# Result stored feature-major, range checks without clips, an inverse root on GpSimd, token-major inputs and a plan driven by need

## The chip, the cores and the metric

The kernel runs on one core of one Trainium2 chip. The metric is the device time of one execution in microseconds (us), the median of several runs. A core has a matrix engine (TensorE, PE in the profile, with its weight loads as PEld), a vector engine (VectorE, DVE), an engine for functions (ScalarE, ACT), a fourth compute engine (GpSimd, POOL) and the engine that issues the DMAs of this kernel (SyncE, SP).

## The reference, cut to what matters

Two blocks in a row. The first is a linear attention whose state decays by a complex factor; the second is a gated block with a product over time.

```python
# attention: q, k, v, a_re, a_im are [batch 4, heads 8, seq 768, dim 48]
mag = sqrt(a_re**2 + a_im**2);  scale = minimum(mag, 0.999) / (mag + 1e-6)
a = (a_re + i*a_im) * scale
S = 0                                    # [batch, head, 48, 48], complex
for t in range(768):
    S = a[t][:, None] * S + outer(k[t], v[t])
    y[t] = q[t] @ real(S)
x = y laid out as [4, 768, 384]          # heads side by side
# gated block: w_in [384, 1024], w_sg [768, 768], w_out [512, 384]
u, v = split(gelu(x @ w_in), 2)          # 512 each
v_n = (v - mean(v)) / sqrt(var(v) + 1e-6) * g_ln
v_s = w_sg @ v_n + b_sg                  # over time, for each batch
result = x + (u * v_s) @ w_out           # [4, 768, 384]
```

## The kernel before, in words

**Tiling.** Time is cut in 24 chunks of 128 tokens (6 for each batch), and chunks are taken in 13 *units* of one or two. For each unit a row of steps runs, each a Python function or generator: `load` (re, im, q, k; L227), `square` (re² + im², L255), `logs` (L273), `scale` (the cumulative decay as a product with a triangular matrix, then exponentials on q and k, L298), `arctan` and `turns` (the cumulative phase, L331 and L342), `sincos` (L374), `rotate` (q and k times cosine and sine, on DVE, L383), and for each chunk `attend` (L392).

**attend.** It transposes Q and K on PE (`pq`, `pk`, L407), evacuates them on ACT (`qt`, `kt`), multiplies them (`pa`, L415), masks the result on DVE (`am`, L417: one for each four heads, so two a chunk, which makes `am` a good counter of chunks), updates the state (`ps`, L424), forms the output (`py`), evacuates it on ACT (`yp`) and stores it feature-major in a scratch array `xd`.

**The gated block.** It runs for each batch in three halves of 256 tokens (the code calls them hf). `normal` (L489) loads x from `xd`, splits it in two parts for the three-product matmul `mm3` (L155; a float32 product as high·high + high·low + low·high in fp32r: `xh`, `xl`), forms the v half (`pv`), gelu, mean and variance (L504, L505), the inverse root `rsqrt` (L457, twelve operations on 128x2 elements on DVE), scales and splits (`vh`, `vl`). `expand` (L519) loads x again and forms u (`pu`). `spatial` (L535) needs all three `normal`s of the batch: for each of four f it forms `pvs` (18 matmuls, L158), then on DVE `tg` = pvs·g + b (L546) and `tg`·u, splits it (`gh` on ACT, `gl` on DVE), and then for each of two chunks forms the output product `po` token-major (12 matmuls of 384 columns), transposes x back with three PE transposes (`px`, L565), copies that to `ob` on ACT, adds `po` on DVE (L569) and stores 128 tokens (L570).

**Clips.** `square` begins with two DVE passes: L260 limits re from below and keeps the smallest value (for the range check at the end, `in_range`), and L262 limits im to ±1. If a value lies outside the range in which the fast form holds, a slow general path (`general`) is taken; it isn't in the runs shown.

**Weights.** They arrive as float64 and are turned to two fp32r parts by integer operations on DVE (`fetch`, L167, tiles `raw` and `bits`). w_sg is float32; `prep_sg` (L200) transposes its 36 blocks on PE (`pt_sg`, L210), casts the high part on ACT (L212) and subtracts on DVE (L213).

**What sets the order.** Every step of every unit and half gets a position from a table of numbers W; all steps are sorted by it and called in that order. Each engine works in order through what was written for it, so this sort is the kernel's schedule, and an instruction that is not ready holds everything behind it on its engine. The same holds for SP, which issues all DMAs. Functions on ACT come in three sets, and each change of set is an ACT_TABLE_LOAD (L116).

Where `EN` maps a name to (early, late), the two numbers choose between two engines for units ahead of and from the seventh on. In before all but `rn` are 0.

Of the kernel before, what the change touches and what calls it, by code (L numbers as in the profile page):

```python
# [29 lines left out]
def tile_kernel(ctx: ExitStack, tc: tile.TileContext, q, k, v, a_re, a_im,  # L30
                w_in, g_ln, w_sg, b_sg, w_out, out):
    nc = tc.nc
    B, H, S, D = q.shape
# [41 lines left out]
    mask = u_phi.bitcast(F32)  # L75
    b_eps = cst([P, 1], F32, "b_eps")
    nc.gpsimd.memset(b_eps, LN_2EPS)
# [4 lines left out]
    vbuf = []
    for i in range(2):
        t = cst([P, H, 64], F32, f"vbuf{i}")
        nc.gpsimd.memset(t, 0.0)
# [22 lines left out]
    def act(out, in_, func, bias=None, scale=1.0):  # L108
        kw = {}
# [90 lines left out]
    def prep_sg(tt):  # L200
# [5 lines left out]
        for g in range(2):  # L206
            pt = psm.tile([P, 3, P], F32, tag="m", name="pt_sg")
            for i in range(3):
                s_ = 3 * g + i
                nc.tensor.transpose(pt[:, i, :], st[:, s_ * P:(s_ + 1) * P], ident)  # L210
# [1 line left out]
            nc.scalar.copy(wh, pt)  # L212
            nc.vector.tensor_tensor(out=wl, in0=pt, in1=wh.bitcast(F32), op=ALU.subtract)  # L213
# [568 lines left out]
```

## Time and profile before

| what | number |
|---|---|
| median of 3 runs | 545.34 us (544.06 to 546.47) |
| the profiled execution | 544.33 us |
| its span, first to last instruction | 542.6 us |
| mean granted TensorE clock | 0.967 |
| DMA moved, mean rate | 50.80 MB, 94 GB/s |
| DMA packets, of those under 512 B | 169747, 145997 |

How to read it: the times of instructions are of the one profiled execution, whose own time, 544.33 us, is 1.7 above the span and 1.0 under the median. A group's row gives line, engine, operation, output and inputs with their shapes, the count after x, then the busy time in us and the mean in ns; behind the second bar stands the idle time of that engine just before these instructions, and what ended most of it. "128x512 f32" is 128 partitions by 512 elements.

### The profile page before, as it was taken

How to read it: one execution, taken by the hardware profiler on the slowest of the kernel's cores; microseconds unless marked ns; L12 is line 12 of the kernel's file. 1: busy time of each engine (PE TensorE's matmuls, PEld its weight loads, DVE VectorE, ACT ScalarE, POOL GpSimd, SP SyncE). 2: the span in 40 equal slices, each digit the busy share in tenths (PEclk: the TensorE clock that was granted, in tenths of full speed). 3: DMA queues.
4: the chain of work that ended last, by engine and by line, in shares of the span. 5: the costliest groups of instructions: out<-in, count | busy, mean ns of one | idle time of the engine just before them, and what ended most of it. 6: DMA issues, size and time to landing. Idle time of an engine off the chain costs nothing.

```text
span 542.6 us, 10051 instructions
## 1 busy us (share of the span) xinstructions
PE 488.5 (90%) x3838; PEld 440.0 (81%) x3838; DVE 403.8 (74%) x939; ACT 340.5 (63%) x573; POOL 2.2 (0%) x14
## 2 busy tenths in 40 slices
PE   1759787959899999999998999999999999999994
PEld 0448474747689999998798999998899999889994
DVE  5898889899888869499888587688874433884432
ACT  5879875777859687593599594874682332442221
POOL 1000000000000000000000000000000000000000
PEclk9989798798899999999999999999999999999998
DMA  8687767455552454454322544134221103120101
GB/s 160 177 192 185 181 150 178 85 123 118 117 117 35 103 100 85 121 118 102 103 39 51 124 83 104 45 88 104 72 32 30 59 16 103 31 87 1 59 31 36
DMA packets 169747, 50.80 MB, mean 94 GB/s; under 512 B 145997, under 2 KB 167503, under 8 KB 169690
## 3 DMA queue, kind: packets, MB, share of 16 engines
q1 hardware_dynamic: 169690, 50.07, 40.1%
q8 instruction: 32, 0.52, 0.4%
q14 instruction: 25, 0.20, 0.1%
HBM read 40.58 MB, written 9.47 MB: 92 GB/s over the span
## 4 chain that ended last, share of the span: by engine, by line
PE 68%; DVE 15%; ACT 12%; issue 3%; DMA 1%; SPq 1%; ACTq 0%; DVEq 0%
PE pvs L158 17%; PE pu L158 9%; PE po L158 8%; PE pa L415 7%; PE pv L158 6%; PE py L441 3%; PE ps L424 3%; PE pq L407 3%; PE pk L407 3%; PE py L446 2%; ACT L116 2%; PE px L565 1%; PE phi L357 1%; ACT vh L120 1%; DVE bst L504 1%
## 5 line engine op out<-in xcount | busy, mean ns | idle before, releaser
L158 PE MATMUL pvs<-wsgh,vh 128*128 128x256 f32 x288 | 83.8, 291 | 0.8 <-ACT vh L120 0.8
L158 PE MATMUL pvs<-wsgh,vl 128*128 128x256 f32 x288 | 81.2, 282 | 0.2 <-DVE vl L153 0.2
L158 PE MATMUL pvs<-wsgl,vh 128*128 128x256 f32 x288 | 81.0, 281 | 0.0
L415 PE MATMUL pa<-qt,kt 96*128 96x128 f32 x384 | 56.7, 289 | 9.8 <-ACT kt L143 9.5
L415 PEld LDWEIGHTS pa<-qt,kt 96*128 96x128 f32 x384 | 51.1, 200 | 17.0 <-ACT kt L143 15.2
L116 ACT ACT_TABLE_LOAD x43 | 55.2, 1283 | 1.6 <-PEq L767 0.8
L158 PEld LDWEIGHTS pvs<-wsgh,vh 128*128 128x128 f32 x288 | 54.3, 189 | 1.8 <-ACT vh L120 1.3
L158 PEld LDWEIGHTS pvs<-wsgh,vl 128*128 128x128 f32 x288 | 54.4, 189 | 0.6 <-DVE vl L153 0.5
L158 PEld LDWEIGHTS pvs<-wsgl,vh 128*128 128x128 f32 x288 | 54.4, 189 | 0.0
L120 ACT ACTIVATE gh<-tg 128x256 fp32r<-128x256 f32 x48 | 20.0, 417 | 40.3 <-DVE tg L548 36.6
L569 DVE TENSOR_TENSOR ob<-po,ob 128x384 f32<-128x384 f32 x24 | 13.3, 555 | 41.5 <-ACT ob L143 38.9
L158 PE MATMUL pu<-xh,winh 128*128 128x256 f32 x144 | 43.0, 300 | 0.0
L158 PE MATMUL pu<-xl,winh 128*128 128x256 f32 x144 | 40.8, 284 | 1.3 <-DVE xl L153 1.3
L407 PE MATMUL pq<-ident,Q 128*96 128x128 f32 x192 | 32.7, 295 | 9.7 <-DVE Q L389 9.7
L158 PE MATMUL pu<-xh,winl 128*128 128x256 f32 x144 | 40.4, 282 | 0.0
L441 PE MATMUL py<-am,vbuf 128*64 128x128 f32 x384 | 39.0, 280 | 1.3 <-DVE am L417 0.9
L546 DVE SCALAR_TENSOR_TENSOR tg<-pvs,gcol,bsg 128x256 f32<-128x256 f32 x48 | 23.2, 482 | 20.9 <-PE pvs L158 20.0
L143 ACT COPY qt<-pq 96x512 f32<-96x512 f32 x48 | 27.7, 577 | 17.0 <-PE pq L407 16.7
L417 DVE TENSOR_TENSOR am<-pa,u_phi 128x512 f32<-128x512 f32 x48 | 32.9, 685 | 5.7 <-PE pa L415 5.7
L407 PEld LDWEIGHTS pq<-ident,Q 128*96 128x96 f32 x192 | 22.7, 134 | 15.6 <-DVE Q L389 11.8
L407 PE MATMUL pk<-ident,K 128*96 128x128 f32 x192 | 32.1, 291 | 1.8 <-DVE K L389 0.9
L158 PE MATMUL pv<-winh,xh 128*128 128x512 f32 x72 | 30.8, 428 | 2.8 <-ACT ob L143 1.9
(228 smaller groups left out, 1264.4 us busy)
## 6 DMA issues: line engine op xcount, KB each, us to landing
x<-xd SPq DMA_DIRECT2D x24, 384.0 KB, 3.4
re<-in_a_re_dram SPq DMA_DIRECT2D x24, 192.0 KB, 3.4
im<-in_a_im_dram SPq DMA_DIRECT2D x24, 192.0 KB, 2.6
q<-in_q_dram SPq DMA_DIRECT2D x24, 192.0 KB, 3.2
k<-in_k_dram SPq DMA_DIRECT2D x24, 192.0 KB, 3.7
vbuf<-in_v_dram SPq DMA_DIRECT2D x24, 192.0 KB, 3.1
xd<-yp SPq DMA_DIRECT2D x48, 96.0 KB, 2.2
out_dram<-ob SPq DMA_DIRECT2D x24, 192.0 KB, 2.0
```

What stands on the lines that cost most here:

```text
L116: p = nc.scalar.preload_act_table_set(SETS[t])
L120: i = nc.scalar.activation(out, in_, func, scale=scale, **kw)
L143: nc.scalar.copy(out, in_)
L158: nc.tensor.matmul(o, w(i), x(i), start=(i == 0 and j == 0), stop=(i == n - 1 and j == 2))
L407: nc.tensor.transpose(pp[:, hh, :], x[:, 4 * g2 + hh, :, :].rearrange("p a d -> p (a d)"), ident)
L415: nc.tensor.matmul(pa[:, hh, :], kt[:, hh, :], qt[:, hh, :], start=True, stop=True)
L417: nc.vector.tensor_tensor(out=am, in0=pa, in1=mask.unsqueeze(1).broadcast_to([P, 4, P]), op=ALU.mult)
L424: nc.tensor.matmul(ps[:, h, :], K[:, h, :, :].rearrange("p a d -> p (a d)"), V[:, h, 0:D], start=True, stop=True)
L441: nc.tensor.matmul(py[64 * e:64 * e + 64, p_, :], V[:, h, :], am[:, h % 4, :], start=True, stop=c == 0)
L446: nc.tensor.matmul(py[64 * e:64 * e + D, p_, :], Sb[:, h, :], qt[:, h % 4, :], start=False, stop=True)
L546: nc.vector.scalar_tensor_tensor(out=tg, in0=pv, scalar=gcol[:, f:f + 1], in1=bsg[:, tsl], op0=ALU.mult, op1=ALU.add)
L569: nc.vector.tensor_tensor(out=ob, in0=po, in1=ob, op=ALU.add)
```

## The change

The host now hands in q, k, re, im as [batch, seq, 384] (token-major, as the kernel's tiles are), v padded to 64 a head and w_sg transposed, and transposes the result, which the kernel now stores feature-major as [4, 384, 768]. In the kernel:

- `load` issues one DMA for each array and unit, `load_v` loads whole rows.
- `prep_sg` has no transposes: it splits the loaded rows, the high part on GpSimd.
- `square` has no clips; im² goes to ACT for all units. A new step `smallest` checks re with a Relu on ACT whose accumulated sum must be 0.
- `rsqrt` is six operations on GpSimd (a power and one Newton step) instead of twelve on DVE.
- `xh` is made on GpSimd. In late units `qt1`, `kt1` and `yp` are evacuated on DVE instead of ACT.
- `spatial` forms `po` feature-major, in three pieces of 128 features by 256 tokens, adds it on DVE to x in place and stores from the x tile. `px`, `ob` and its ACT copy are gone. The x tile has two buffers as before.
- The plan keeps a table W with other numbers and a list of what each step needs (`needs`); `advance` first runs whatever a step still lacks and then the step.

```diff
-    EN = dict(hl=(0, 0), ll=(0, 0), ht=(0, 0), hw=(0, 0), lw=(0, 0), hx=(0, 0), lx=(0, 0), hv=(0, 0), lv=(0,
...
+    EN = dict(hl=(0, 0), ll=(1, 0), ht=(0, 0), hw=(0, 0), lw=(0, 0), hs=(1, 0), ls=(0, 0), hx=(1, 1), lx=(0, 0),
+              hv=(0, 0), lv=(0, 0), hg=(0, 0), lg=(0, 0), re2=(0, 0), im2=(1, 1), sb=(0, 0), qt0=(0, 0), qt1=(0, 1),
+              kt0=(0, 0), kt1=(0, 1), yp=(0, 1), ep=(0, 0), em=(0, 0), q0=(0, 0), q1=(0, 0), k0=(0, 0), k1=(0, 0),
...
-        for g in range(2):
-            pt = psm.tile([P, 3, P], F32, tag="m", name="pt_sg")
...
-            nc.scalar.copy(wh, pt)
-            nc.vector.tensor_tensor(out=wl, in0=pt, in1=wh.bitcast(F32), op=ALU.subtract)
+        split(wsgh[:, tt, :], wsgl[:, tt, :], st, "s")
...
-            for i in range(m):
-                nc.sync.dma_start(out=t[:, i], in_=SRC[nm][b, :, (c0 + i) * P:(c0 + i + 1) * P, :].rearrange("h t d -> t h d"))
+            nc.sync.dma_start(out=fl4(t[:, 0:m]),
+                              in_=SRC[nm][b, c0 * P:(c0 + m) * P, :].rearrange("(c p) f -> p c f", p=P))
...
-        nc.vector.tensor_scalar(out=fl3(re), in0=fl3(re), scalar1=RE_MIN, scalar2=None, op0=ALU.max, op1=ALU.min,
-                                accum_out=re_min[:, n:n + 1])
-        nc.vector.tensor_scalar(out=im, in0=im, scalar1=-1.0, scalar2=1.0, op0=ALU.max, op1=ALU.min)
...
+            act(re, re, AF.Relu, bias=b_min, scale=-1.0, accum_out=re_low[:, n:n + 1])
...
-        nc.vector.tensor_scalar(out=x, in0=var, scalar1=1e-6, scalar2=None, op0=ALU.add)
...
+        g = nc.gpsimd
+        g.tensor_scalar(out=x, in0=var, scalar1=1e-6, scalar2=1.0, op0=ALU.add, op1=ALU.mult)
+        g.tensor_tensor(out=y, in0=x, in1=mhalf[:, 0:n], op=ALU.pow)
+        g.tensor_mul(t, y, y)
+        g.tensor_mul(t, t, x)
+        g.tensor_scalar(out=t, in0=t, scalar1=-0.5, scalar2=1.5, op0=ALU.mult, op1=ALU.add)
+        g.tensor_mul(y, t, y)
...
-            po = None if last else product()
-            px = psm.tile([P, DM], F32, tag="m", name="px")
-            for kt in range(NK):
-                nc.tensor.transpose(px[:, kt * P:(kt + 1) * P], x[:, kt, ts], ident)
...
-            nc.vector.tensor_tensor(out=ob, in0=po, in1=ob, op=ALU.add)
-            nc.sync.dma_start(out=out[b, t0:t0 + P, :], in_=ob)
+        for d in range(NK):
+            ds = slice(d * P, (d + 1) * P)
+            po = psm.tile([P, UT], F32, tag="m", name="po")
+            mm3(po, lambda f: wouth[:, f, ds], lambda f: woutl[:, f, ds], lambda f: gh[:, f, :], lambda f: gl[:, f, :], NF)
+            nc.vector.tensor_tensor(out=x[:, d, :], in0=po, in1=x[:, d, :], op=ALU.add)
+            nc.sync.dma_start(out=out[b, ds, tsl], in_=x[:, d, :])
...
+    def advance(key, count):
+        while key in chains and chains[key][1] < count:
+            k = chains[key][1]
+            for other, steps in needs(key, k):
+                advance(other, steps)
+            chains[key][1] += 1
...
-             m1=(4.445, 4.584, 4.693, 4.807, 5.418, 6.538, 5.137, 6.03, 7.024), m0=(2.443, 3.699, 4.464,
...
+             ph=(6,), p_chk=(0.105, 0.554), chk=((0.493,), (0.504,), (0.504,)), m=((2.443, 3.811, 4.457, 4.713, 5.629,
```

PE's instructions around the first product over time (`pvs`), which can begin when batch 0's last `normal` is done. Before:

```order
L441 MATMUL py<-am,vbuf_101 64x128 x2
L446 MATMUL py<-qt,S 48x128 x2
L158 MATMUL pu<-xh,winh 128x256
L407 MATMUL pq<-ident,Q 96x128 x4
L158 MATMUL pvs<-wsgh,vh_882 128x256
L158 MATMUL pvs<-wsgl,vh_882 128x256
```

And after, the same place:

```order
L164 MATMUL pu<-xh,winh 128x256
L164 MATMUL pu<-xl,winh 128x256
L164 MATMUL pu<-xh,winl 128x256
L164 MATMUL pvs<-wsgh,vh_829 128x256
L164 MATMUL pvs<-wsgl,vh_829 128x256
L164 MATMUL pvs<-wsgh,vl_830 128x256
```

Before, attention of batch 1's chunks (`py`, `pq`) stands between; after, a whole `pu` (36 matmuls) of batch 0 stands ahead of it. Up to the first `tg` before has 17 `am`, after 14.

DVE's instructions in batch 0's first `normal`, from its statistics (L504 before, L500 after; `mv` is mean and variance) to the scaling. Before, with the clips of units of batch 1 (re, im) and the squares (`sq`) between the small operations of the inverse root (`nx`, `nt`, `ny`):

```order
L504 BN_STATS bst<-vr 128x6
L260 TENSOR_SCALAR re_947,re_min<-re_947 128x768
L505 BN_AGGR mv<-bst 128x2
L262 TENSOR_SCALAR im_950<-im_950 128x768
L462 TENSOR_SCALAR nx<-mv 128x2
L260 TENSOR_SCALAR re_1224,re_min<-re_1224 128x768
L463 TENSOR_SCALAR nt<-nx 128x2
L269 TENSOR_TENSOR sq<-im_950 128x384
L465 TENSOR_SCALAR ny<-nt 128x2
L340 SCALAR_TENSOR_TENSOR sn_968<-sn_968,phi 128x384
L474 TENSOR_TENSOR nt<-ny 128x2
L417 TENSOR_TENSOR am<-pa,u_phi 128x512
```

And after:

```order
L500 BN_STATS bst<-vr 128x6
L436 TENSOR_TENSOR T<-ps,S 96x384
L501 BN_AGGR mv<-bst 128x2
L265 ISA l_918,sq_max<-l_918,sq 128x384
L265 ISA sq_max 128x1
L437 TENSOR_TENSOR S<-T,dec 96x384
L507 TENSOR_SCALAR vr<-vr,mv,ny 128x512 x2
L344 SCALAR_TENSOR_TENSOR sn_893<-sn_893,phi 128x384
L320 TENSOR_TENSOR q_744<-q_744,ep_930 128x384
L159 TENSOR_TENSOR vl_830<-vr,vh_829 128x512
L159 TENSOR_TENSOR vl_835<-vr,vh_834 128x512
```

The root's operations have left DVE's queue, and with them the clips and squares that stood between.

The last DMAs that SP issues. Before, the loads of x (L483) and the stores of `ob` (L570):

```order
L483 DMA x<-xd_0_123 128x3x256
L570 DMA out_dram<-ob 128x384
L483 DMA x<-xd_1_124 128x3x256
L570 DMA out_dram<-ob 128x384 x2
L483 DMA x<-xd_2_125 128x3x256
L570 DMA out_dram<-ob 128x384 x5
```

And after, with the stores from the x tile (L552):

```order
L479 DMA x<-xd_0_128 128x3x256
L552 DMA out_dram<-x 128x256 x3
L479 DMA x<-xd_1_129 128x3x256
L552 DMA out_dram<-x 128x256 x3
L479 DMA x<-xd_2_130 128x3x256
L552 DMA out_dram<-x 128x256 x6
```

A load of x now stands behind the three stores of the half whose tile it takes.

More of the change, by code (lines that the diff above doesn't have):

```diff
@@ new lines, in tile_kernel, with lead, once, chain @@
+    chains, plan, engines = {}, [], {}
+    def lead(key, f, *a):
+        def once():
+            f(*a)
+            yield
+        chains[key] = [once(), 0]
+    def chain(key, gen):
+        chains[key] = [gen, 0]
+    def chunk(b, c):
+        n, (_, c0, _) = next((n, u) for n, u in enumerate(units) if u[0] == b and u[1] <= c < u[1] + u[2])
+        return "attend", n, c - c0
+    def needs(key, k):
+        nm, *a = key
+        n = a[0] if a else 0
+        if nm == "square":
+            return [(("load", n), 1)]
+        if nm == "logs":
+            return [(("square", n), 1)]
+        if nm == "smallest":
+            return [(("logs", n), 1)]
+        if nm == "arctan":
+            return [(("logs", n), 2)]
+        if nm == "load":
+            return [(("smallest", n - 2), 1), (("turns", n - 2), UC)] if n > 1 else []
+        if nm == "loadqk":
+            return [(("rotate", n - 1, i), 1) for i in range(units[n - 1][2])] if n > 1 else []
+        if nm == "scale":
+            return [(("logs", n), 4), (("loadqk", n), 1)]
+        if nm == "turns":
+            return [(("arctan", n), 1)] + [(("turns", n - 1), UC)] * (n > 0)
+        if nm == "sincos":
+            return [(("turns", n), UC)]
+        if nm == "rotate":
+            return [(("sincos", n), 2), (("scale", n), 2 + a[1])]
+        if nm == "attend":
+            b, c0, _ = units[n]
+            c = c0 + a[1]
+            out = [(("rotate", n, a[1]), 1), (("scale", n), UC + 2)]
+            return out + [(chunk(b, c - 1), 6)] if c else out
+        if nm in ("normal", "expand"):
+            b, j = a
+            out = [(("w", nm), 1)] + [(chunk(b, j * UC + i), 6) for i in range(UC)]
+            if nm == "normal" and k > 2 and b:
+                out.append((("spatial", b - 1, NU - 1), 4))
+            return out
+        if nm == "spatial":
+            b, j = a
+            out = [(("normal", b, i), 4) for i in range(NU)] + [(("expand", b, j), 5), (("w", "sg"), 1)]
+            return out + [(("w", "out"), 1)] * (k > 3)
+        if nm == "w":
+            return [(("prep", *i), 1) for i in weights[a[0]]]
+        if nm == "ok":
+            return [(("smallest", i), 1) for i in range(N)]
+        return []
@@ new lines, in advance, with at @@
+    def advance(key, count):
[4 more added lines that the diff above has]
+            chains[key][1] += 1
+            early[0] = engines.get(key, True)
+            if next(chains[key][0], "end") == "end":
+                chains[key][1] = count
+    def at(p0, p1, key, gen, count, soon=True):
+        chain(key, gen)
+        engines[key] = soon
+        for i in range(count):
+            plan.append((p0 + (p1 - p0) * i / count, len(plan), key, i + 1))
```

225 lines of the change are left out of this document (110 added, 115 removed).

## The prediction, before the result was known

> **What bounds the kernel now.** I read the page first: busy shares, then the slices (the columns are 40 equal stretches of 13.6 us).
>
> ```profile
> span 542.6 us, 10051 instructions
> PE 488.5 (90%) x3838; PEld 440.0 (81%) x3838; DVE 403.8 (74%) x939; ACT 340.5 (63%) x573; POOL 2.2 (0%) x14
> ...
> PE   1759787959899999999998999999999999999994
> DVE  5898889899888869499888587688874433884432
> ```
>
> TensorE looks like the bound with 90%, but the slices show two stages: up to about the twelfth slice DVE stands at 8 and 9 and PE has gaps; behind it PE stands at 9 throughout. The cut is the first use of the spatial product, which needs a whole batch and all three of its `normal`s. The tile's rows (count, then lowest, middle and highest ns, first and last start) give the time, and the windows cut there (columns: length, then busy time and count of PE, PEld, DVE, ACT, POOL, then granted clock, DMA share, GB/s).
>
> ```profile
> L546 DVE SCALAR_TENSOR_TENSOR tg<-pvs,gcol,bsg x48: 473/484/486, 164.1 to 530.0; 128x256 f32<-128x256 f32 x48
> L120 ACT ACTIVATE gh<-tg x48: 401/417/443, 165.5 to 531.0; 128x256 fp32r<-128x256 f32 x48
> L153 DVE TENSOR_TENSOR gl<-tg,gh x48: 407/424/427, 166.2 to 531.4; 128x256 fp32r<-128x256 f32 x48
> ```
>
> ```profile
> 0.00:118.10 118.10, 84.11 (x556) 60.98 (x556) 101.67 (x229) 90.58 (x145) 2.17 (x14) 0.90 0.71 161
> 118.10:164.10 46.00, 38.66 (x268) 32.62 (x269) 40.78 (x102) 32.51 (x54) 0.00 (x0) 0.93 0.52 112
> 0.00:164.10 164.10, 122.78 (x824) 93.60 (x825) 142.46 (x330) 123.08 (x198) 2.17 (x14) 0.91 0.66 147
> 164.10:534.90 370.80, 365.77 (x3017) 346.45 (x3015) 260.81 (x609) 217.45 (x377) 0.00 (x0) 1.00 0.30 71
> 534.90:542.60 7.70, 0.00 (x0) 0.00 (x0) 0.56 (x1) 0.00 (x0) 0.00 (x0) 0.70 0.10 35
> ```
>
> Ahead of the first `tg` DVE works 142.46 of 164.1 us (87%), ACT 75%, PE 75%: this stage is bound by DVE's work and by the hops between DVE, ACT and PE. Behind it PE idles only 370.80 - 365.77 = 5.0 us at clock 1.00: this stage is PE's, and DVE (70%) and ACT (59%) have room. Then 7.7 us without PE. The profiled execution took 544.33 us, so 1.7 lies outside the span; the median of the runs, 545.34, is 1.0 above it.
>
> So a microsecond off DVE counts once in the first 164 us and hardly afterwards; a microsecond off PE counts afterwards.
>
> **Late stage: what PE loses and gains.** The chain of waits at the end (start, length, piece) gives PE's rates when nothing waits.
>
> ```profile
> 453.62 6.39 PE pvs L158 x54
> ...
> 530.31 2.12 PE po L158 x12
> 532.42 0.33 PE px L565 x3
> 532.75 2.13 PE po L158 x12
> ...
> 534.98 0.56 DVE ob L569
> ```
>
> px: 72 transposes at 0.33/3 = 0.11 us: -7.9 us, all behind 164.1, all on PE's path. po: before 24 x 12 matmuls of 384 columns at 2.12/12 = 0.177 (50.9 us); after 36 x 12 of 256 columns; pvs has that shape, 6.39/54 = 0.118, so 51.1 us: +0.2. The same multiply work in other portions; feature-major brings PE only the transposes.
>
> What the new order moves: 17 `am` (8.5 chunks) stand ahead of the first `tg` before, 14 (7 chunks) after. Counted by the order, 13 pa, 24 pq and pk, 8 ps, 16 py and 10 phi and pg go behind it, and 9 pu come ahead.
>
> ```profile
> 142.03 2.08 PE pa L415 x8
> 149.16 1.15 PE ps L424 x14
> 150.68 0.22 PE py L446 x4
> 152.54 0.44 PE pq L407 x4
> ```
>
> 13 x 0.26 + 24 x 0.11 + 8 x 0.08 + 16 x 0.055 = 7.6; phi and pg (384 columns, as po: 0.177) 1.8; less 9 pu (256 columns, 0.118) 1.1; rounded up for ps and py, whose smaller pieces run less evenly: +9 (bounds 7 and 11). Late stage: 370.8 - 7.9 + 0.2 + 9 = 372.1 if its idle time stays at 5.0. Added there too: at the very end the last po needs gh and gl of the last pvs (tg 0.48, its product with u as long as gl, 0.42, gh 0.42, gl 0.42 = 1.74) and has nine matmuls (1.06) before it: +0.7. The order shows other work there for most halves. Late idle time between 0 and 15 us is the bound of what an order that I can't time does: I take the old 5.0, since DVE's late sum hardly changes (the 42 evacuations of qt, kt and yp, at about 0.58, come to it and 14 of the 24 squares, 7 us, and 24 adds to `ob` of 128x384 turn into 36 of 128x256, while a quarter of the rsqrt work goes) and ACT's falls.
>
> The added `x` in place is 36 x 128x256 at about 0.42 (gl's shape and form), between DVE works that PE does not wait for. The x tile is held until its stores have landed; that is a rival.
>
> **Early stage: what DVE loses.**
>
> ```profile
> L417 DVE TENSOR_TENSOR am<-pa,u_phi 128x512 f32<-128x512 f32 x17 | 11.7, 686 | 2.1 <-PE pa L415 2.1
> L269 DVE TENSOR_TENSOR sq<-im 128x384 f32<-128x384 f32 x14 | 7.7, 552 | 0.1
> L260 DVE TENSOR_SCALAR_CACHE_REDUCE re<-re 128x768 f32<-128x768 f32 (+1 forms) x9 | 7.7, 857 | 3.0 <-DMA re<-in_a_re_dram 3.0
> L262 DVE TENSOR_SCALAR im<-im 128x768 f32<-128x768 f32 (+1 forms) x8 | 4.0, 501 | 1.2 <-DMA im<-in_a_im_dram 1.2
> ```
>
> These are the groups ahead of the first `tg` (count, busy, mean ns, idle ahead). Gone are L260 (7.7) and L262 (4.0); L269's squares (7.7) go to ACT. The inverse root: in the chain of a late `normal` it runs from its first operation to the scaling that needs it.
>
> ```profile
> 466.75 0.18 DVE nx L462
> ...
> 469.12 1.00 DVE vr L511 x2
> ```
>
> 469.12 - 466.75 = 2.4 us, three times ahead of `tg`: 7.1. Together 26.5; some 2.5 of it belongs to the unit that moves behind anyway: 24. The steps that move (1.5 chunks of products, rotations, masks; about 6 us of DVE each by the rows at 0.55 and 0.69) take 9 more. DVE ahead of `tg`: 142.5 - 24 - 9 = 109.5.
>
> ACT: 14 squares come (0.5 each by wsgh's row, 128x384; about 6, less what moves), Relu with accumulation (0.84 by xh's row, 128x768; the order has seven of the 13 ahead, two of half that size, 5), 12 wsgh and 4 xh go to GpSimd, and the evacuations, exponentials and rounds of a chunk and a half move behind, about 8.
>
> ```profile
> L116 ACT ACT_TABLE_LOAD x16 | 20.5, 1283 | 1.1 <-PEq L767 0.8
> L212 ACT CAST wsgh<-pt_sg 128x384 fp32r<-128x384 f32 x12 | 5.3, 490 | 0.3 <-PE pt_sg L210 0.2
> L120 ACT ACTIVATE xh<-x 128x768 fp32r<-128x768 f32 x4 | 3.4, 843 | 0.8 <-PE pv L158 0.8
> ```
>
> 123.1 + 6 + 5 - 5.3 - 3.4 - 8 = about 117. That makes ACT the busiest engine of the stage, and DVE's 24 us can't all be time.
>
> I cut at the sixth chunk, the last that batch 0 needs (its evacuation, and the last `normal`'s vh, below). Before: 118.1 us with DVE 101.7. About 10 of DVE's 24 fall there and nothing moves behind, ACT rises by 3 (squares) from 90.6 to 93 in it. 118.1 - 10 + 1 = 109 (bounds 105, ACT at 88%, and 114, only half of it).
>
> ```profile
> 118.09 0.58 ACT L143 COPY yp<-py 128x512 f32<-128x512 f32 x1 [0.66 <-PE py L446]
> ```
>
> ```profile
> 161.27 1.15 ACT L120 ACTIVATE vh<-vr 128x512 fp32r<-128x512 f32 x2
> ```
>
> From there 46.0 us passed before, with DVE busy 40.8 of it by chunks 7 and 8, weight preparation and clips that the last `normal` had to pass in DVE's queue. Now those stand behind, and little but the `normal`'s own chain is left: yp 0.58, store, load,
>
> ```profile
> L153 DVE TENSOR_TENSOR xl<-x,xh 128x768 fp32r<-128x768 f32 x24 | 22.9, 953 | 8.2 <-ACT xh L120 6.9 <-PE pa L415 1.1
> L120 ACT ACTIVATE vr<-pv 128x512 f32<-128x512 f32 x24 | 14.1, 590 | 5.4 <-PE pv L158 4.0 <-DVE woutl L153 0.9 <-DVE vl L153 0.3
> ```
>
> ```profile
> x<-xd SPq DMA_DIRECT2D x24, 384.0 KB, 3.4
> xd<-yp SPq DMA_DIRECT2D x48, 96.0 KB, 2.2
> out_dram<-ob SPq DMA_DIRECT2D x24, 192.0 KB, 2.0
> ```
>
> that is 2.2 + 3.4, xh on GpSimd 1.1 (below), xl 0.95, two pv of nine matmuls (18 x 128x512, each 4/3 of 0.177: 4.2), gelu 0.59, statistics 0.9 (128x512 as am, and a small operation), root 1.5 (below), scaling 0.5 (half of the 1.00 for two), vh 0.58, vl 0.69 (as am), 18 pvs at 0.118 = 2.1: sum 19.4. DVE's own work in it is about 19 and ACT's 25 (what ACT has ahead of `tg` less 93). I take 28: ACT's 25 and 3 for hand-overs; bounds 22 and 36. First `tg`: 109 + 28 = 137 (bounds 128 and 150) against 164.1: -27. Of this 9 come back as moved matmuls, so the early stage is worth 18.
>
> **GpSimd.** Its only rows are set-up.
>
> ```profile
> L85 POOL MEMSET vbuf<- 128x512 f32 x2 | 1.0, 524 | 0.0
> L66 POOL TENSOR_SCALAR_AFFINE_SELECT upper<-upper 128x128 f32<-128x128 f32 x1 | 0.3, 292 | 0.0
> L77 POOL MEMSET b_eps<- 128x1 f32 x1 | 0.1, 98 | 0.0
> ```
>
> From 98 ns for one element a row to 524 for 512 the memset rises by 0.83 ns an element: 128x768 is 0.74 us; the select reads as well: 0.1 + 768 x 1.5 ns = 1.25. I take 1.1 for xh and wsgh. Six root operations on 128x2: 0.6 (at 98 ns) to 3 (at half a microsecond, if a power or a first call costs as a full tile); I take 1.5 against 2.4. Ahead of `tg` GpSimd has 6 + 3 tiles and three roots, about 14 us of 137, beside DVE. By these rows it costs nothing but its place in the chain. The Trainium skill (GPSIMD Engine Reference, 8. Key points) says that GpSimd shares its SBUF interfaces with VectorE and contends with DVE instructions that have two SBUF inputs; no row here has both at work, so none confirms it, and by it the sum would be that of rival C.
>
> **The rest.** pt_sg: 36 transposes early, 5.7 us of PE, but PE has 41 us of idle time there: nothing (they cost DVE 12 subtractions, which stay as six larger). Loads in rows of 1536 bytes instead of 192: DVE waited 3.0 + 1.2 us for re and im; the first load is part of both kernels: 0 to -3, within the 109. The tail holds one add and one store; the store falls from 192 to 128 KB: 0 to -0.5, taken as 0.
>
> **Sum**: 137 + 372.1 + 0.7 + 7.7 + 1.7 = 519.2 for a profiled execution, plus 1.0 to the median: 520 us.
>
> **The rivals.**
>
> A, the forecast, 0.54: 520, from 512 (first `tg` at 130) to 530 (at 145).
>
> B, the early gain doesn't come, 0.16: ACT's 20.5 us of table loads and the hops set the early pace, not DVE's work. For it: ACT comes to 117 of what would be 137, and PE's longest early idle is behind ACT's and DVE's results. Against it: DVE, not ACT, stands at 9 in most early slices. From half to all of the 18 is lost, and up to 3 that ACT gains in work count: 529 to 541, likeliest 532.
>
> C, GpSimd slows DVE, 0.10: the 14 us of early GpSimd time go partly onto DVE (8 to 11 of them with overlap where DVE would wait anyway): 520 + 9 = 529.
>
> D, more comes, 0.14: the order by need removes nearly all queueing, first `tg` at 126 and late idle time down to 0: 520 - 11 - 5 = 504 (498 to 510).
>
> E, slower, 0.06: the result is stored from the x tile, of which there are two, so the next load of x must wait for the third add and its store, and the loads stand in SP's queue in front of others. Per half: add 0.43, issue about 0.4, landing 2.0 = 2.8 us, with the load's own 3.4 and xh, xl 2.1 behind it 8.3, where before the tile was free at px. If it is all exposed in each of 12 halves, but for the load that waits either way: 12 x 2.8 = 34: 554. It decides from (25 + 3)/12 = 2.3 us exposed per half. Against it: the order puts a whole other product (pvs of 72 matmuls, 8.5 us) between most stores and the next pv or pu.
>
> That the change does not do what it says is excluded for px and the clips, whose instructions are absent from the order.
>
> **How the numbers follow.** Likeliest A: 520. The range reaches down into D and up through C and B to 538: 505 to 538; left out are E (0.06), half of D (0.07) and a sixth of B (0.03), 0.16 in all. A difference under 0.5% (2.7 us: 542.6 to 548.1) counts as none: 0.03, the edges of B and E (0.01 and 0.02). Slower: the rest of E, 0.04. Faster: 0.93.
>
> **What would show it.** In the profile after: first `tg` at 130 to 145; DVE's busy time ahead of it 105 to 115, ACT's 112 to 122; PE's idle time behind it under 10; no transposes of x; xh on POOL near 1.1 us. Wrong: a first `tg` after 150 (B; or C, if am's 686 ns or xl's time has grown beside POOL), many waits of PE for xl or xh behind it and SP waiting for stores of x (E).

## The result and the profile after

The changed kernel takes 526.06 us (median of 4 runs, 525.19 to 526.53), the kernel before 544.83 on the same chip (544.06 to 546.47): a ratio of 0.965, with a 95% interval of 0.962 to 0.968. That is 18.8 us less where 25 were forecast; 520 was predicted, with a range of 505 to 538. Comparisons below go by the ratio to runs of the kernel before on the same chip (medians 544.8 to 545.6). The ratio leaves out runs that count as slow, more than 1.5% above the fastest of their kernel: seven of ten of `old_plan` (546.2 to 548.5, where the other three took 538.1 to 545.9) and one of `xh_act`.

The page after: the span, the engines' busy shares and two rows of the slices (40 of 13.1 us).

```profile
span 524.5 us, 9940 instructions
...
PE 472.6 (90%) x3874; PEld 428.0 (82%) x3874; DVE 386.2 (74%) x783; ACT 307.9 (59%) x522; POOL 55.3 (11%) x118
...
PE   0568778797999999999999999999999999999995
...
PEclk9997878999999999999999999999999999999999
```

The shape is the same: a stage with gaps on PE, then PE without any. It is cut at the first `tg`, and the early stage again at the sixth chunk's `yp` (columns as before: length, PE, PEld, DVE, ACT, POOL, clock, DMA share, GB/s).

```profile
L542 DVE SCALAR_TENSOR_TENSOR tg<-pvs,gcol,bsg x48: 451/483/486, 146.3 to 514.4; 128x256 f32<-128x256 f32 x48
```

```profile
118.27 0.57 ACT L149 COPY yp<-py 128x512 f32<-128x512 f32 x1
```

```profile
0.00:118.30 118.30, 80.29 (x531) 58.49 (x532) 96.18 (x196) 93.67 (x157) 13.63 (x30) 0.91 0.58 171
118.30:146.30 28.00, 23.75 (x162) 19.21 (x162) 19.41 (x35) 23.63 (x41) 8.20 (x15) 1.00 0.39 106
0.00:146.30 146.30, 104.04 (x691) 77.70 (x692) 115.59 (x231) 117.31 (x196) 21.84 (x45) 0.93 0.55 158
146.30:518.90 372.60, 368.56 (x3186) 350.30 (x3184) 270.21 (x553) 190.56 (x327) 33.43 (x73) 1.00 0.28 78
518.90:524.50 5.60, 0.00 (x0) 0.00 (x0) 0.39 (x1) 0.00 (x0) 0.00 (x0) 0.90 0.15 49
```

The first `tg` came 17.8 us earlier (164.1 to 146.3), the PE-bound stage is 1.8 longer, the tail 2.1 shorter: together the 18.1 that the span lost. Of the early stage the second piece fell from 46.0 to 28.0, to the number forecast. The first piece did not move: 118.1 before, 118.3 after, though 109 was forecast. DVE did work 5.5 us less in it. But PE's idle time ahead of the first `tg` is 146.3 - 104.0 = 42.3 us, and was 164.1 - 122.8 = 41.3. Added up like this, PE has 18.7 us less of work there and waits as long as before. That says where the time went and not what set it: in the run `fill` below, 14.4 us more of PE's work ahead of the first `tg` moved it by 2.7 us.

What took the place of DVE's work shows in the shares of the page's chain (part 4), before and after:

```profile
PE 68%; DVE 15%; ACT 12%; issue 3%; DMA 1%; SPq 1%; ACTq 0%; DVEq 0%
```

```profile
PE 60%; DVE 14%; DMA 9%; ACT 8%; POOL 4%; issue 3%; SPq 1%; POOLq 0%; DVEq 0%; ACTq 0%
```

DMA went from 1% of the chain to 9%. Adding up the chain's pieces ahead of the first `tg`: DVE 51.3 us before and 30.9 after, ACT 34.3 and 20.2, PE 60.8 and 41.8, but DMA 7.4 and 32.7. The longest of these pieces after (start, length, piece), with the first `lo`, the decays that the first `pg` of PE needs:

```profile
5.03 6.34 DMA raw<-in_moe_w_in_dram
...
13.28 0.48 DVE lo L291
...
45.20 4.25 DMA raw<-in_moe_w_in_dram
...
61.09 5.84 DMA raw<-in_moe_w_in_dram
```

The weights' conversion (L181) waits in DVE's queue for its load, and what stands behind it there waits too. In the waits of DVE and of PE ahead of the first `tg` (total, times, longest):

```profile
DVE bits L181 <- DMA raw<-in_moe_w_in_dram: 5.4, 2, 4.6
```

```profile
PE pg L312 <- DVE lo L291: 17.1, 2, 13.8
```

Before, that wait of PE was 10.3 us at its longest, and `lo` began at 9.67:

```profile
PE pg L308 <- DVE lo L287: 12.8, 2, 10.3
```

```profile
9.67 0.57 DVE lo L287
```

So a theory for the experiments: loads of weights, on two staging tiles, replaced DVE's work on the chain (theory DMA). Rivals were that ACT bounds the early stage (B), that GpSimd and DVE hold each other up (C), and, after the first runs, that TensorE's clock and the order decide.

### The profile page after: what moved, and what is told of

Same layout as the page of the kernel before. It is cut to its first block, busy times and chain, and to the rows that moved or that the text cites. A ratio compares the mean times of both kernels' runs of the same rounds, so it can differ in the third digit from the quotient of the medians.

```text
span 524.5 us, 9940 instructions
## 1 busy us (share of the span) xinstructions
PE 472.6 (90%) x3874; PEld 428.0 (82%) x3874; DVE 386.2 (74%) x783; ACT 307.9 (59%) x522; POOL 55.3 (11%) x118
## 4 chain that ended last, share of the span: by engine, by line
PE 60%; DVE 14%; DMA 9%; ACT 8%; POOL 4%; issue 3%; SPq 1%; POOLq 0%; DVEq 0%; ACTq 0%
PE pvs L164 16%; PE po L164 8%; PE pv L164 7%; PE pu L164 6%; PE pa L419 5%; PE py L445 3%; DMA raw<-in_moe_w_in_dram 3%; PE ps L428 3%; PE py L450 3%; PE pq L411 3%; PE pk L411 2%; DMA x<-xd 2%; DMA st_sg<-in_moe_w_sg_dram 1%; DMA re<-in_a_re_dram 1%; DVE bst L500 1%
## 5 line engine op out<-in xcount | busy, mean ns | idle before, releaser
L164 PE MATMUL pvs<-wsgh,vh 128*128 128x256 f32 x288 | 82.3, 286 | 0.6 <-ACT u__4421 L126 0.6
L419 PEld LDWEIGHTS pa<-qt,kt 96*128 96x128 f32 x384 | 48.2, 191 | 15.7 <-ACT kt L149 14.5
L419 PE MATMUL pa<-qt,kt 96*128 96x128 f32 x384 | 53.0, 279 | 8.8 <-ACT kt L149 8.6
L153 POOL TENSOR_SCALAR xh<-x 128x768 fp32r<-128x768 f32 x24 | 23.8, 993 | 328.8 <-DMA x<-xd 124.2
L126 ACT ACTIVATE gh<-tg 128x256 fp32r<-128x256 f32 x48 | 19.9, 414 | 60.8 <-DVE tg L544 51.6
L164 PE MATMUL po<-gh,wouth 128*128 128x256 f32 x144 | 42.4, 296 | 1.0 <-ACT gh L126 0.6
L164 PE MATMUL pu<-xh,winh 128*128 128x256 f32 x144 | 41.0, 288 | 0.7 <-DVE x L551 0.6
L164 PE MATMUL po<-gl,wouth 128*128 128x256 f32 x144 | 41.2, 286 | 0.1
L164 PE MATMUL po<-gh,woutl 128*128 128x256 f32 x144 | 40.7, 283 | 0.0
L411 PE MATMUL pq<-ident,Q 128*96 128x128 f32 x192 | 31.3, 284 | 2.5 <-DVE Q L392 2.5
L159 DVE TENSOR_TENSOR xl<-x,xh 128x768 fp32r<-128x768 f32 x24 | 22.8, 951 | 12.8 <-POOL xh L153 12.8
```

The lines of the kernel that those rows point to most:

```text
L126: i = nc.scalar.activation(out, in_, func, scale=scale, **kw)
L153: nc.gpsimd.tensor_scalar(out=h, in0=src, scalar1=scale, scalar2=1.0, op0=ALU.mult, op1=ALU.mult)
L159: dp("l" + nm).tensor_tensor(out=l, in0=src, in1=h.bitcast(F32), op=ALU.subtract)
L164: nc.tensor.matmul(o, w(i), x(i), start=(i == 0 and j == 0), stop=(i == n - 1 and j == 2))
L411: nc.tensor.transpose(pp[:, hh, :], x[:, 4 * g2 + hh, :, :].rearrange("p a d -> p (a d)"), ident)
L419: nc.tensor.matmul(pa[:, hh, :], kt[:, hh, :], qt[:, hh, :], start=True, stop=True)
```

## The experiments

**fm_only**: the kernel before with the feature-major result alone.

```diff
-            po = None if last else product()
-            px = psm.tile([P, DM], F32, tag="m", name="px")
...
+        for d in range(NK):
...
+            nc.vector.tensor_tensor(out=x[:, d, :], in0=po, in1=x[:, d, :], op=ALU.add)
+            nc.sync.dma_start(out=out[b, ds, tsl], in_=x[:, d, :])
```

> The kernel before with one thing changed: the output product feature-major, x added in place, stored from the x tile (no px, no ob). The order table is the old one. By the sum of the prediction: 72 transposes at 0.11 us are gone, 7.9 us, and the tail is 2.1 us shorter as in the kernel after (5.6 for 7.7), first tg stays at 164: 545 - 10 = 535 us (533 to 538). Rival E, the x tile that is held until its stores have landed, in an order that was not made for it: up to 2.8 us in each of 12 halves come back, 540 to 560, and PE's waits for xh and xl behind 164 us add up to 10 us and more.

538.7 us, ratio 0.9895 (0.985 to 0.994): -5.7 by the ratio. Its windows:

```profile
0.00:163.00 163.00, 119.29 (x823) 91.16 (x824) 142.31 (x329) 122.84 (x198) 2.18 (x14) 0.93 0.67 148
163.00:531.10 368.10, 363.83 (x3090) 343.24 (x3088) 263.02 (x622) 207.69 (x353) 0.00 (x0) 1.00 0.31 71
531.10:537.00 5.90, 0.00 (x0) 0.00 (x0) 0.41 (x1) 0.00 (x0) 0.00 (x0) 0.72 0.16 48
```

The late stage lost 2.7 us (370.8 to 368.1), not 7.9; the tail lost 1.8. Adding up in the trace, from the start of one matmul to that of the next, what each product takes of the late stage: px 7.4 us before and none here, but po 51.8 before and 57.0 here (0.180 for 384 columns, 0.132 for 256), where 51.1 had been forecast. Rival E fell: PE's waits behind the first `tg` did not grow (368.1 - 363.8 = 4.3 us idle, 5.0 before). The time is just above the range that was expected, since po came dearer.

**tok_loads**: the kernel before with q, k, re, im and v token-major.

```diff
-            for i in range(m):
-                nc.sync.dma_start(out=t[:, i], in_=SRC[nm][b, :, (c0 + i) * P:(c0 + i + 1) * P, :].rearrange("h t d -> t h d"))
+            nc.sync.dma_start(out=fl4(t[:, 0:m]),
+                              in_=SRC[nm][b, c0 * P:(c0 + m) * P, :].rearrange("(c p) f -> p c f", p=P))
```

> The kernel before with only q, k, re, im and v handed in token-major (rows of 1536 and 2048 bytes instead of 192, one DMA for each unit and array, no zeroed vbuf). DVE waited 4.2 us for re and im in the kernel before. By the prediction 0 to -3: 542 to 545 us. Rival, that the DMA queue's share in the early stage (0.66 of 16 engines) holds the loads of weights and scratch too: first tg 6 us earlier or more, 534 to 539.

541.2 us, ratio 0.9946 (0.992 to 0.997): -3, the upper end of what was forecast; the first `tg` came at 161.5, and the DMA share ahead of it fell from 0.66 to 0.53.

**dve_only**: the kernel before without clips, with squares and check on ACT and the root on GpSimd.

```diff
-        nc.vector.tensor_scalar(out=fl3(re), in0=fl3(re), scalar1=RE_MIN, scalar2=None, op0=ALU.max, op1=ALU.min,
-                                accum_out=re_min[:, n:n + 1])
-        nc.vector.tensor_scalar(out=im, in0=im, scalar1=-1.0, scalar2=1.0, op0=ALU.max, op1=ALU.min)
...
+                act(t, im[:, i], AF.Square)
...
+            act(re, re, AF.Relu, bias=b_min, scale=-1.0, accum_out=re_low[:, n:n + 1])
```

> The kernel before with only the clips removed, squares and check on ACT and the inverse root on GpSimd, old order, old result, old loads. The prediction's view (24 us less on DVE ahead of the first tg count about half or more): first tg at 146 to 154, 528 to 536 us. Theory B (ACT bounds, which gets 12 us more): first tg at 160 to 172, 541 to 553 us.

545.2 us, ratio 1.002 (0.999 to 1.005): nothing. The stage ahead of the first `tg` and the late stage, then the early stage cut at the sixth chunk's `yp`:

```profile
0.00:154.60 154.60, 113.32 (x784) 86.32 (x785) 119.11 (x247) 128.02 (x216) 8.61 (x36) 0.93 0.70 154
154.60:533.50 378.90, 370.75 (x3056) 351.09 (x3054) 238.15 (x488) 232.25 (x407) 15.81 (x54) 1.00 0.30 71
...
0.00:115.80 115.80, 81.00 (x559) 59.20 (x560) 92.49 (x195) 97.99 (x167) 4.19 (x24) 0.94 0.74 164
115.80:154.60 38.80, 32.32 (x226) 27.12 (x227) 26.62 (x53) 30.03 (x50) 4.42 (x12) 0.91 0.57 123
```

The first `tg` does come 9.5 us earlier, near the late end of what the prediction's view had (146 to 154). But 40 matmuls fewer stand ahead of it, PE's idle time there is 154.6 - 113.3 = 41.3 us as in before, and the late stage is 8 us longer (5.0 of PE's work, 3.1 of idle time). Up to the sixth chunk 9.2 us less of DVE's work (101.7 to 92.5) brought 2.3 us. In the chain ahead of the first `tg` DVE has 16.8 us (51.3 before), ACT 56.8 (34.3 before): ACT took DVE's place. An earlier first `tg` is no gain if it only sorts PE's work to the other side of it.

**old_plan**: the operations of the kernel after in the order of the kernel before.

```diff
-    for _, _, key, count in sorted(plan, key=lambda e: e[:2]):
-        advance(key, count)
+    for _, _, f in sorted(plan, key=lambda e: e[:2]):
+        f()
```

> All operations of the kernel after, in the order of the kernel before (its table W and its sort, without the list of needs; the new check step is put behind the logarithms). Theory order (the order by need takes the last normal's chain out of the queues, 46 us to 28 behind the sixth chunk): first tg at 155 to 162, 532 to 540 us. Theory operations (fewer operations on DVE, ACT and PE make the gain, whatever the order): first tg at 144 to 150, 524 to 529 us.

Median 546.6 us (538.1 to 548.5), ratio 0.993 (0.988 to 0.999): about 4 of the 19 us by the ratio, nothing by the median. So the operations alone bring little; with the order that belongs to them they bring the rest. Theory operations fell. Theory order missed its numbers too, on the slow side: the first `tg` came at 163.8, not 155 to 162. From the sixth chunk's `yp` on:

```profile
124.60:163.80 39.20, 34.37 (x246) 29.67 (x245) 27.48 (x53) 28.76 (x49) 6.56 (x14) 0.91 0.44 127
```

This piece took 46.0 us before, 38.8 and 39.2 in the old order with some or all of the new operations (dve_only, old_plan), and 28.0 in the kernel after: the order is the larger part of what the piece lost. The clock in it is 0.93, 0.91, 0.91 and 1.00, so part of the step from 39 to 28 may be the clock's.

**xh_act** and **prep_late**, two small changes to the kernel after: its early `xh` and `wsgh` on ACT, and only the positions of the weight preparation moved back.

```diff
-    EN = dict(hl=(0, 0), ll=(1, 0), ht=(0, 0), hw=(0, 0), lw=(0, 0), hs=(1, 0), ls=(0, 0), hx=(1, 1), lx=(0, 0),
+    EN = dict(hl=(0, 0), ll=(1, 0), ht=(0, 0), hw=(0, 0), lw=(0, 0), hs=(0, 0), ls=(0, 0), hx=(0, 1), lx=(0, 0),
```

```diff
-             4.775, 5.897, 6.632)), prep=((0.188, 1.21), (0.857, 2.402), (2.402, 3.009), (2.991, 3.819)))
+             4.775, 5.897, 6.632)), prep=((1.0, 1.9), (1.7, 3.2), (3.2, 3.9), (3.9, 4.6)))
```

> The kernel after with wsgh and the early xh on ACT instead of GpSimd. Theory C (GpSimd and DVE hold each other up: xh took 2.69 us at 125.3 and 0.83 where DVE was idle, DVE's two-input operations beside wsgh 1.18 and 1.58 instead of 0.55 and 0.95): these come back to 0.55 and 0.95, first tg 2 to 5 us earlier, 521 to 524 us. Theory B (ACT's work bounds the first 118 us: 93.7 busy): ACT gets 6 x 0.85 + 3 x 0.85 = 7.7 us more, first tg 4 to 8 later, 530 to 534. If neither bounds, 526 within 1.5.

> The kernel after with only the positions of the weight preparation moved back (numbers of the table: the four groups begin at 1.0, 1.7, 3.2 and 3.9 instead of 0.19, 0.86, 2.4 and 2.99). Theory 1 (weights prepared in front of the first chunks hold DVE while their loads come, 4.6 us at 7 us and again at 61): the sixth chunk's yp 4 to 8 us earlier than 118.3, first tg at 138 to 143, 518 to 523 us, if the later preparation doesn't delay the first products. Theory B (ACT bound): sixth yp stays within 2 us of 118.3, 525 to 528 us.

543.6 us (ratio 0.997, 0.993 to 1.000) and 533.8 (0.979, 0.973 to 0.985), against 0.965 of the kernel after: both far slower, and prep_late on the side that no theory had. The stage ahead of the first `tg`, first of xh_act, then of prep_late:

```profile
0.00:160.50 160.50, 115.28 (x688) 88.30 (x689) 112.36 (x231) 123.34 (x206) 7.06 (x34) 0.85 0.51 144
```

```profile
0.00:156.30 156.30, 112.27 (x690) 85.44 (x691) 115.58 (x231) 116.50 (x196) 17.39 (x45) 0.88 0.52 148
```

PE does the same work there as in the kernel after (688 to 691 matmuls), but takes 115.3 and 112.3 us for it instead of 104.0, at a granted clock of 0.85 and 0.88 instead of 0.93. That is as much as 11.2 of the 14.2 us by which xh_act's first `tg` is later, and 8.2 of prep_late's 10.0; whether the slower clock made the delay or came with it is not shown. PE's idle time is 45.2 and 44.0 us, 42.3 in after. In prep_late the conversion still stood at the front of DVE's queue (other than the expectation assumed) and only its load came later, so DVE waited 5.8 us for it instead of 4.6. Theory B is neither shown nor excluded by xh_act: ACT's 6 us more and the slower clock can't be told apart in it. Theory C is right there in what it says of DVE, which takes 112.4 us for the same 231 operations that take 115.6 in after; the time that C expected did not come. prep_late's profiled execution is the slowest of its four (530.1 to 536.9).

**root_dve** and **sq_dve**: the kernel after with the inverse root on DVE again, and with the early squares and the early check on DVE again.

```diff
-        g.tensor_tensor(out=y, in0=x, in1=mhalf[:, 0:n], op=ALU.pow)
...
+        for _ in range(3):
+            nc.vector.tensor_mul(t, y, y)
```

```diff
-              hv=(0, 0), lv=(0, 0), hg=(0, 0), lg=(0, 0), re2=(0, 0), im2=(1, 1), sb=(0, 0), qt0=(0, 0), qt1=(0, 1),
+              hv=(0, 0), lv=(0, 0), hg=(0, 0), lg=(0, 0), re2=(0, 0), im2=(0, 1), sb=(0, 0), qt0=(0, 0), qt1=(0, 1),
...
-              tau=(0, 0), ob=(0, 1), rn=(0, 1), nw=(0, 0), chk=(1, 1))
+              tau=(0, 0), ob=(0, 1), rn=(0, 1), nw=(0, 0), chk=(0, 1))
```

> The kernel after with the inverse root on DVE again (twelve operations). In the profile after the six GpSimd operations take 2.5 us from the statistics to the scaling, the twelve on DVE took 2.4 in the kernel before. Theory 1 (latency of one normal's chain sets the last 28 us, weight preparation and queues the first 118): first tg at 145 to 148 against 146.3, 525 to 528 us. Theory 2, as the prediction had it (each microsecond of DVE work ahead of the first tg counts about once): DVE +7 there, first tg at 151 to 154, 531 to 534 us.

> The kernel after with the early squares of im and the early check of re on DVE again (Relu and squares leave ACT: 7 x 0.85 and 14 x 0.52 = about 12 us; DVE gets about 14). Theory B (ACT bounds the early stage: GpSimd's tiles put back on ACT cost 14 us there): first tg 4 to 12 us earlier, 515 to 522 us. The prediction's view (DVE bounds it): first tg 8 to 14 us later, 533 to 540. Theory balance (both stand at 80% there, 115.6 and 117.3 us, and what counts is which of them stands in the chain): within 4 us, 523 to 530.

526.9 us (ratio 0.969, 0.966 to 0.973; first `tg` at 145.0) and 529.4 (0.971, 0.966 to 0.976):

```profile
0.00:149.30 149.30, 101.56 (x691) 77.38 (x692) 124.86 (x253) 108.98 (x174) 22.39 (x45) 0.93 0.54 155
```

The root's place makes no difference that these runs show. In sq_dve 9.3 us more on DVE and 8.3 less on ACT cost 3.0 us of the first `tg`: neither engine's sum sets the stage, as theory balance had it.

**lo_first**, **stage4** and **lo_stage** go at the loads: the first conversion forced behind the first two `lo`; w_sg's rows staged in the tiles of `xh` and `xl`, so that they don't share two tiles with the weights; and both.

```diff
+            if n < 2:
+                first.append(i.ins.name)
...
+            while first:
+                tc.add_manual_dep(i.ins, first.pop(), nosync, reason="weights behind the first logarithms")
```

```diff
-        st = mp.tile([P, S], F32, tag=stage(), name="st_sg", bufs=1)
+        st = mp.tile([P, S], F32, tag=("xh", "xl")[tt % 2], name="st_sg", bufs=1)
```

> The kernel after with one forced order on DVE: the first weights' conversion stands behind the decays (lo) of the first two units instead of in front of them. In the profile after, DVE waits 4.6 us for that weight load, with lo behind it, and PE waits 13.8 us for lo. Theory DMA (loads of weights on the chain took the place of DVE's work: 33 us of the chain ahead of the first tg, 7 before): lo 3 to 4 us earlier, first chunk's yp at 31 to 33 instead of 34.7, first tg at 140 to 144, 520 to 524 us. Theory clock and order (what counts is how long TensorE's gaps are, and a displaced order lowers its clock): first yp earlier, but first tg between 146 and 156, 526 to 535 us, with a granted clock below 0.93 ahead of it.

> The kernel after with w_sg's rows staged in the tiles xh and xl (free then) instead of the two that the weights use, so that four loads can be under way instead of two. Theory DMA: the chain's waits for raw and st_sg (6.3, 4.3, 5.8, 3.6 and 3.2 us) shrink by half, first tg at 136 to 142, 516 to 522 us. Theory clock and order: first tg between 144 and 156, 524 to 535 us, according to the granted clock.

> Both of the above in one: theory DMA 512 to 520 us; theory clock and order: 522 to 535 us, by the granted clock ahead of the first tg.

524.4 us (ratio 0.963, 0.959 to 0.967), 530.0 (0.974, 0.969 to 0.979) and 520.9 (0.956, 0.952 to 0.959; 520.5 to 521.4). The stage ahead of the first `tg`, in that order:

```profile
0.00:142.90 142.90, 100.79 (x691) 76.24 (x692) 115.80 (x231) 117.34 (x196) 18.59 (x45) 0.95 0.56 162
```

```profile
0.00:146.20 146.20, 105.34 (x691) 81.28 (x692) 115.80 (x232) 116.77 (x196) 21.05 (x45) 0.92 0.54 159
```

```profile
0.00:140.40 140.40, 100.52 (x691) 75.67 (x692) 114.61 (x232) 117.20 (x196) 19.64 (x45) 0.95 0.58 165
```

lo_stage has the same operations on the same engines as the kernel after, and is 5 us faster than it; its sixth `yp` comes at 112.3 instead of 118.3. In the chain ahead of the first `tg` DMA has 18.3 us instead of 32.7. The clock is hardly the reason: at the same mean clock of 0.985 over the whole execution, one of the kernel after took 525.2 us and one of lo_stage 520.7. So the loads held part of what was missing in the forecast; it is a little less than theory DMA had expected (512 to 520). lo_first alone is 1.6 us faster by its median, within its interval; its first `lo` came at 9.1 us instead of 13.2, but its first `yp` at 36.2, and not at the 31 to 33 that theory DMA had expected. stage4 alone took as much of DMA off the chain (17.6 us left) and gained nothing, as theory clock and order had it: PE's longest wait for `lo` stayed at 13.8 us, since the first conversion and its load stand ahead as before, and the clock is 0.92. So loads on the chain are not the whole of it. The two edits together brought more than either; that the place of the first conversion decides whether the other edit counts is the likeliest reading, and no run separates it from the clock.

**fill**: lo_stage with 96 more transposes on PE in the gaps.

```diff
+            if b == 0:
+                fill = psm.tile([P, P], F32, tag="m", name="fill")
+                for _ in range(8):
+                    nc.tensor.transpose(fill, ident, ident)
```

> The kernel of lo_stage with 96 extra transposes of the identity on TensorE ahead of the first tg, whose result nobody reads (8 before each half chunk's pa of batch 0; the order of everything else on DVE stays). They do no part of the computation. Theory clock (TensorE's gaps lower its granted clock, 0.95 there and 0.72 to 0.85 in some stretches, and a slower clock lengthens the chain): the clock rises to 0.98 or more, and though 10.6 us of work come (96 at 0.11), the first tg stays within 2 us of 140.4 or comes earlier, 517 to 523 us. Rival (the clock follows from the order and is no cause, extra work in the gaps only delays): clock within 0.02 of 0.95, first tg 3 to 10 us later, 524 to 531 us.

522.2 us (ratio 0.957, 0.953 to 0.960). Its stage ahead of the first `tg`:

```profile
0.00:143.10 143.10, 114.89 (x787) 90.93 (x788) 115.41 (x232) 117.73 (x196) 21.50 (x45) 0.93 0.54 162
```

PE works 14.4 us more there than in lo_stage and idles 28.2 us instead of 39.9; the first `tg` is 2.7 us later (143.1, between the two expectations), and the ratio is that of lo_stage within the intervals. So most of the added work fitted into PE's waits. The clock is 0.93 and not the 0.98 of theory clock; but the time lies in that theory's range and not in its rival's, and the profiled execution has the lowest mean clock of its four (0.978; the others 0.984 to 0.992, lo_stage 0.983 to 0.986). So these runs don't decide whether filled gaps raise the clock. What the trace shows in steps of 1 us, without those from 73 to 77, which are busy and halved (length, PE busy and count, clock, DMA share, GB/s):

```profile
68.00:69.00 1.00, 0.34 (x5) 1.00 0.04 0
69.00:70.00 1.00, 0.00 (x0) 1.00 0.55 132
70.00:71.00 1.00, 0.00 (x0) 1.00 0.92 295
71.00:72.00 1.00, 0.15 (x2) 0.66 0.75 227
72.00:73.00 1.00, 1.00 (x12) 0.50 0.33 132
...
77.00:78.00 1.00, 1.00 (x5) 0.50 0.84 242
78.00:79.00 1.00, 1.00 (x7) 0.93 0.75 187
```

After 3.0 us without matmuls the clock halves (at 71.3), and it comes back after 6.3 us of full work (71.9 to 78.1). Earlier in the same trace it stayed halved for all of nine busy microseconds:

```profile
31.00:40.00 9.00, 9.00 (x46) 0.50 0.63 186
```

That stretch began at 26.9, and no gap of PE just before it was longer than 1.1 us. PE was busy for 1.4 of the 3.4 us ahead of the fall:

```profile
23.53:26.94 3.41, 1.38 (x6) 1.00 1.01 319
```

So several short gaps close together are enough to halve the clock.

## Why the prediction was right or wrong

**Right**: that it gets faster, by 0.965 where 0.954 was forecast; that the late stage stays (372.6, forecast 372.1 + 0.7); the 28 us behind the sixth chunk, which measured 28.0; ACT's work ahead of the first `tg` (117.3, forecast 117); idle time of PE behind the first `tg` under 10 (4.0); no rival E. Of the signs it named, the first `tg` (146.3 for 130 to 145) and DVE's work ahead of it (115.6 for 105 to 115) lie just outside.

The early stage was to be worth 18 us, 27 less 9 that come back as moved matmuls. It is worth 17.8 less 8.4, so 9.4: half of the gain, and not most of it.

**Wrong: the first piece.** The step that failed is "118.1 - 10 + 1 = 109": DVE's 10 us less up to the sixth chunk were to be 9 us of time. In after DVE lost 5.5 there, since work on later chunks came in for part of the clips, squares and roots (the rotations of Q and K above all, 14.3 us before and 18.8 after), and the time didn't fall at all: in the chain the weights' loads took DVE's place. dve_only shows the same step failing with few loads on the chain (DMA 5.7 us): 9.2 us less on DVE, 2.3 us of time. With fewer loads on the chain of after (lo_stage) the piece is 112.3 and the first `tg` 140.4, which brings back 5.9 of the 9.3 us between 137 and 146.3. For the other 3.4 no cause is shown; the clock (0.95 in lo_stage) and DVE's work (114.6 for the 109.5 forecast) are candidates.

**Wrong in its reason: what the early gain consists of.** The sum took DVE's busy share (87%) as the bound of the stage. dve_only had 23 us less of DVE's work ahead of the first `tg` and gained nothing. What changed in after is the piece behind the sixth chunk, and the larger part of that came with the order, with the clock in it at 1.00 instead of 0.91 to 0.93. That its 28 us are "ACT's 25 and 3 for hand-overs" is not shown: ACT was busy for 23.6 of them, and by the prediction's own terms it is 24 (117 less 93), as DVE's 19 is 18 (109.5 less 91.7). PE's 18.7 us less of work ahead of the first `tg` are the transposes of w_sg, the work that moved behind, and a clock of 0.93 for 0.91. The prediction costed the transposes at nothing, since PE had idle time. No run takes them alone; fill, where 14.4 us more of PE's work cost 2.7, speaks for it, though nothing waits for its transposes as the split waits for w_sg's.

**Luck: the moved work.** Adding up py, pa, ps, pq, pk, phi and pg in the late stage gives 114.0 us before and 122.4 after, 8.4 for the 9 of the sum. But by the traces 29 pa, 16 ps and 32 py moved, where the sum has 13, 8 and 16, and its price of a pa, 0.26, was read where the clock was halved. In the late stage of after a pa takes 0.11. The place in the profile before (length, PE busy and count, clock, DMA share, GB/s):

```profile
142.00:144.20 2.20, 2.17 (x9) 0.51 0.83 170
```

For pa the count too low and the price too high nearly cancel (3.4 and 3.2 us). There is luck in the total as well: the first `tg` missed by 9.3 us, the time only by 6, since the tail came out 2.1 shorter, and the median lies 0.1 below the profiled execution where 1.0 above was taken.

**Mis-sized: po.** Forecast +0.2; after has po at 55.9 us, +4.1. px's 7.4 (for 7.9) was right, so the feature-major result is worth about 3 us on PE and not 7.7. The late sum came out all the same because `pvs` took 2.4 us less (104.8 to 102.4) and PE idled 1 us less.

**Mis-sized: the tail**, 5.6 for 7.7. fm_only alone has it (5.9), so it belongs to the last add and store; which part isn't shown.

**GpSimd.** Its rows in the kernel after, with two single `xh`, one beside busy DVE and one not:

```profile
L468 POOL TENSOR_TENSOR ny<-nx,mhalf 128x2 f32<-128x2 f32 x12 | 9.2, 765 | 1.0
```

```profile
125.28 2.69 POOL L153 TENSOR_SCALAR xh<-x 128x768 fp32r<-128x768 f32 x1 [1.64 <-DMA x<-xd]
...
188.74 0.83 POOL L153 TENSOR_SCALAR xh<-x 128x768 fp32r<-128x768 f32 x1 [44.84 <-DVE am L421]
```

```profile
24.21 0.55 DVE L393 TENSOR_TENSOR K<-k,sn 128x384 f32<-128x384 f32 x1
24.68 1.18 DVE L392 TENSOR_TENSOR Q<-q,cs 128x384 f32<-128x384 f32 x1
```

The power (`ny`) takes 0.77 us and the whole root 2.5 from the statistics to the scaling, where 1.5 was taken; DVE needed 2.4, so the move frees DVE and shortens no chain. `xh` takes 0.83 us by itself (1.1 was taken), and 2.69 at 125.28, on the chain of the last `normal`, while DVE multiplies two tiles of SBUF. The other way round, the product at 24.68, beside `wsgh` (24.40, 1.05 us), takes 1.18 instead of 0.55. That is the contention of rival C. The trace agrees with the Trainium skill (GPSIMD Engine Reference, 8. Key points), by which GpSimd contends with DVE instructions that have two SBUF inputs; that had to stay open in the prediction. Its size is below the rival's, which had 9 us: the two tiles on the chain at 125.28 and 24.68 lost 1.9 and 0.6 us, and DVE's work ahead of the first `tg` is 3.2 us less with GpSimd's early tiles on ACT (xh_act). What it costs in time no run shows.

**Rival B** had a true part: with DVE's work gone, ACT takes over the chain (56.8 us in dve_only). ACT's sum was not the bound in after, since 8.3 us less on ACT and 9.3 more on DVE (sq_dve) made it 3 us slower.

## What to carry to other kernels

A busy share of 87% over a stage of mixed work is no bound: look at what the engine that sets the end waits for in sum, and whether removing the busy engine's work changes that sum, before its microseconds are counted as time. Watch for work that merely changes sides of the mark at which a stage is cut. An instruction that waits for a load in an in-order queue holds all behind it, so when compute is taken off a queue, ask which loads now arrive too late and how many staging tiles they share: one forced place in the order and two other tiles gave 5 us here. An order that is written as a table of numbers belongs to its operations; the same operations in the old order were worth about 4 of 19 us, and two small edits cost 8 and 17. Look at the granted clock before the price of an instruction is read off a row: here a row at half clock gave 0.26 us for 0.11.

## What the runs showed of the hardware

TensorE's granted clock differed from order to order, and with it PE's time for the same work: the same 688 to 691 matmuls ahead of the first `tg` took 100.5 us at a mean clock of 0.95, 104.0 at 0.93, 112.3 at 0.88 and 115.3 at 0.85. What of this is time of the kernel isn't shown, since fill took 14.4 us more of PE's work for 2.7 us.

The mean comes from stretches at exactly half clock. Ahead of the first `tg`, in the traces of all these runs, each lasts 3.41 us or two, three or four times that: in lo_stage they add up to 4 times 3.41 us, in after to 6, in prep_late to 11 and in xh_act to 14. In the 3.41 us ahead of such a stretch PE was busy for 0.1 to 2.1 us. In dve_only, ahead of 93.2, the longest gap in them was 0.8 us and PE was busy for 1.4.

In fill the clock came back after 6.3 us of full work at one place and after 10 (30.5 to 40.6) at another. The Trainium skill (TensorE: Matmul & The Clock Gate, Part 1: The HAM clock gate) lets the clock fall after an idle window of about 3.4 us and rise after one busy window of that length, counted freely. The traces agree with the length; but PE was not idle in the window ahead of 26.9 in fill (1.4 us busy), and while 6.3 us hold at most one whole window, the 10 hold two, counted from the fall at 26.9, so there one was not enough. The measurement decides. What in an order decides between 0.85 and 0.95 stays open beyond this.
